# A planned transformer block on one NeuronCore: another written-out issue order, with the second norm's scale and shift of chunk 3 done for pairs of tiles

## The chip, the cores and the metric

The kernel runs on one core of a Trainium2 chip. Five engines work side by side, each through its own list of instructions in a fixed order: TensorE (PE) does matrix products, VectorE (DVE) and ScalarE (ACT) work element by element, GpSimd (POOL) does a little of the same more slowly, and SyncE (SP) issues nearly all DMA transfers. An instruction starts when its turn in its engine's list has come and the results it needs are there; a late one holds up everything behind it on that engine. The metric is the device time of one execution in microseconds (us), the median of several runs; lower is better.

## The reference, cut to what matters

All tensors are bf16; there are S = 2048 tokens of D = 512 numbers, 32 heads of 16, F = 1792.

```python
sa, ca, ga, sb, cb, gb = six rows of (silu(c) @ w_mod)
h = layernorm(x) * (1 + ca) + sa
q, k, v = split(h @ wqkv)                     # 32 heads of 16
logits[s, w] = q[s] . k[s - 2 * w] / 4        # w = 0..7, masked where s - 2w < 0
x = x + ga * ((softmax(logits) . v[s - 2 * w]) @ wo)
h = layernorm(x) * (1 + cb) + sb
h = layernorm(h)                              # the mixer's own norm
u = gelu(h^T @ w1 + b1)                       # over the tokens: [512, 2048] @ [2048, 1792]
x = x + gb * (u @ w2 + b2)^T
```

Each token attends to eight earlier ones, two apart. The second half mixes the tokens: its first product needs the normed rows of all 2048 tokens before any of its results is complete, and its second product needs all of `u`.

## The kernel before, in words

The 2048 tokens are 16 tiles of 128, and the tiles form five chunks of 2, 4, 4, 4 and 2 tiles (`SIZES`; chunk 0 has tiles 0 and 1, chunk 1 has tiles 2 to 5, chunk 2 tiles 6 to 9, chunk 3 tiles 10 to 13, chunk 4 tiles 14 and 15). `build_chunk` (line 605) lists the operations of one chunk by name. In each name the first number is the chunk or the tile:

- `ln1s`, `rstd1_`, `nb1_`, `n1_`: the first norm. VectorE takes mean and variance of a tile (a statistics instruction and an aggregate), ScalarE makes the reciprocal root of a group, VectorE makes the bias `nb`, and the tile is scaled and shifted (`n1_`) on ACT, DVE or POOL. Which one is written down per tile in the strings `NE` (line 265: first, second and third norm; A, D, P).
- `tr`/`hT` or `xt`: the tile is transposed, by TensorE and copies in chunks 0 and 1, by DMA in chunks 2 to 4.
- `qkv`, `ev`: products with the weights, which `wsc` has scaled by `1 + ca` (column `a1col`, from `modcols1`, from the loaded `ld_wmod1`); results are moved from PSUM to SBUF by `ev`.
- `qk`, `red`, `max`, `sub`, `exp`, `esum`, `rcp`, `smB`: the logits. VectorE multiplies q by the eight shifted k (`qk`, four instructions a chunk, 128x4096 in chunks 1 to 3 and 128x2048 in chunks 0 and 4); TensorE sums over the head's numbers (`red`), and the softmax follows.
- `vd`, `a2`: DMAs that lay out v and the softmax for the next step. `pv`, `pvacc`, `oev`: VectorE multiplies softmax by v, TensorE sums, ACT moves the result. `wo`, `x1`: the output product and the new x.
- `ln2q`, `ln2m`, `rstd2_`, `nb2_`, `n2_`: the second norm (mean and square sums on ACT, `ln2m` turns them into mean and variance on DVE). `aff`: VectorE multiplies by `1 + cb` and adds `sb` (two instructions), for a group of `GRP[ch]` tiles. `ln3s`, `rstd3_`, `nb3_`, `h3_`: the third norm.

The token mixer's first product (`mlp1_<sweep>_<f tile>_<first token tile>`) runs in sweeps over ranges of token tiles (`MIX`), so that TensorE has work on finished tiles while later chunks are still in attention: sweep 0 over tiles 0 to 5 or 0 to 9, parked in SBUF by `park`, later sweeps added by `inj` or `padd`; then `gelu`, and `mlp2` with `fin` and the store `st_out`. The weights of the mixer come in by `ld_w1_` (three buffers in rotation) and `ld_w2_`.

Nothing is scheduled while the kernel is built: `ORDER` (line 182) is the issue order of all operations written out, `schedule` (line 85) follows it, hands out buffers by it (six PSUM banks, four product buffers `big`, five `vD`) and lets every engine's list fall out of it. A token `:a`, `:d` or `:p` picks the engine where there is a choice; `:q` splits a product into four that use 32 columns of the array each; `fill:k:n` puts n small products on TensorE that compute nothing (`warm` does the same). Every instruction is recorded at line 133, the helper that issues it, so the profile is read by tile names and by order.

Of the kernel before, what the change touches and what calls it, by code (L numbers as in the profile page):

```python
# [179 lines left out]


ORDER = """
ld_x_1_2 ident ld_c act_table ld_x_1_4 ld_x0 consts warm2 ld_x_2_8 ld_x1 cps ld_x_2_6 silu_exp ld_wmod1 ln1s3
ld_wqkv1 ln1s5 ld_wqkv0 ld_x_3_10 ln1s4 ln1s2 ln1s0 rstd1_1 ln1s1 ld_wmod0 ln1s9 rstd1_0 nb1_0 nb1_1 silu_dve
n1_1 n1_0 ld_x_4_14 ln1s6 n1_5 n1_2 fill:2:114 tr0_0 ln1s8 modcols1 n1_3 halo0 ld_wqkv2 n1_4 hT0_3:a hT0_1:d
hT0_0:a ld_x_3_12 fill:4:11 tr1_2 a1col hT0_2:d wsc1_0:a wsc1_1:d tr1_0 ld_wo3 wsc1_3:d wsc1_2:d hT1_3:a ln1s7
qkv0_12 hT1_1:a ld_wmod5 wsc0_0:a wsc0_1:d qkv0_10 wsc0_3:d ld_b2 rstd1_2 wsc0_2:d ln1s10 ld_wmod4 hT1_0:a
qkv0_00 ev0_10:a ln1s11 ev0_12:a modcols0 ld_wo0 nb1_2 qkv0_02 sab hT1_2:d ld_wmod3 n1_6 qvb0 ln1s15 qkv1_02
qvb_cp0 ln1s14 wsc2_2 ev0_02:a qvb1 ln1s13 wsc2_3 qkv1_10 wsc2_1:a wsc2_0:a qvb_cp1 qk0_3 qkv1_00 ev0_00:a
qkv0_22 qk0_2 ev1_02:a qkv1_01 ev1_10:a qk0_0 qkv0_20 ev1_01:a qk0_1 ev1_00:a red0_0 xt6 qkv1_12:q n1_9 qk1_0  # L190
ev0_20:a red0_1 red0_2 ld_wo1 red0_3 mask ev1_12:a ld_wmod2 qkv1_13:q n1_7 qkv1_03 max0 n1_8 xt7 qk1_2 qkv1_11
ev1_03:a xt9 sub0 qkv1_23 ev1_11:a exp0 qkv1_21 qk1_1 ev1_13:a xt8 ev0_22:a esum0 qkv1_22:q ld_b1 rcp0 halo_v1:p
rstd1_4 vd0_1 smB0 qkv1_20 qk1_3 a2_0_1 modcol2 a2_0_0 ev1_20:a red1_0 ev1_23:a a2_0_2 red1_1 ev1_22:a red1_2
a2_0_3 ln1s12 red1_3 ev1_21:a ld_wo2 qkv2_00 mcols0 nb1_4 max1 rstd1_3 n1_14 vd0_0 n1_15 qkv2_10 vd0_2 nb1_3
ev2_00:a n1_10 sub1 pv0_1 ev2_10:a xt10 qkv2_01 n1_12 qk2_0 mrowt0 qkv2_02 exp1 vd1_3 qkv2_11 vd0_3 ev2_01:a
n1_11 vd1_2 qkv2_22 pv0_2 ev2_11:a xt12 qkv2_12 mrows0:a ev2_02:a qk2_1 pvacc0_2 xt11 ev2_12:a red2_0 n1_13
esum1:q halo_v2:p xt13 qkv2_13:q rcp1 qk2_2 ev2_22:a qkv2_03:q vd1_1 ev2_13:a qkv2_23:q ev2_03:a smB1 qkv2_20:q
qk2_3 a2_1_3 red2_1 ev2_20:a a2_1_2 qkv3_01:q halo_k3:a ev2_23:a a2_1_0 red2_2 a2_1_1 qkv3_13 pv0_0 ld_w1_0_896
red2_3 st_row0 pv0_3 ev3_13:a qkv2_21:q vd1_0 max2 pvacc0_0 ev2_21:a qkv3_10:q pv1_3 pvacc0_1 sub2:q oev0_0:a
qkv3_23:q ev3_10:a exp2 qkv3_00:q ld_row0 pv1_2 xt14 ev3_01:a qkv3_02:q ev3_00:a qkv3_20:q vd2_0 ev3_23:a vd2_1  # L200
esum2:q pv1_0 ld_w1_0_0 qkv3_21 rcp2 pvacc0_3 qkv3_03:q woq_s oev0_2:a ev3_02:a pvacc1_3 ev3_03:a smB2 qkv3_11:q
pv1_1 a2_2_2 wo1:q ev3_11:a a2_2_1 ev3_21:a wo0 xt15 x1_1 halo_v3:a qk3_1 pvacc1_1 oev1_3:a a2_2_0 pvacc1_0 x1_0
a2_2_3 qkv3_12 oev1_1:a ld_w1_0_512 oev1_0:a qk3_0 pvacc1_2 vd2_2 modcol3 oev1_2:a vd2_3 ev3_12:a ln2q0 wo4
qk3_3 wo5 x1_4 ln2q1 qkv4_12 mcols1 ev3_20:a qk3_2 red3_0 ln2q4 red3_1 qkv3_22:q ln2m0 wo3 ev3_22:a pv2_1 x1_5
mrowt1 wo2:q mrows1:a x1_3 st_row1 red3_2 pv2_0 x1_2 pvacc2_1 rstd2_0 red3_3 ln2q2 qkv4_02:q oev2_1:a ld_row1
nb2_0 max3 n2_0 vd3_3 ev4_02:a vd3_0 pv2_3 sub3 vd3_2 qkv4_10 exp3 pvacc2_0 n2_1 esum3 pv2_2 ln2q3 qkv4_20
ev4_12:a qkv4_22:q rcp3 ev4_20:a ln2m2 pvacc2_2 aff0 warm3 oev2_0:a oev2_2:a qkv4_00:q smB3 rstd2_2 ln2q5 nb2_2
pvacc2_3 ln3s0 a2_3_1 n2_2 warm1 ev4_22:a a2_3_0 ln3s1 n2_3 biascols oev2_3:a a2_3_2 ln2m4 ev4_10:a aff2 wo7:q
a2_3_3 rstd2_4 ld_w2_1 rstd3_0 wo6:q nb2_4 nb3_0 ln3s2 n2_4 n2_5 h3_0 vd3_1 ln3s3 wo8:q h3_1 x1_6 aff4 warm0
rstd3_2 x1_7 wo9:q nb3_2 ln3s4 h3_2 h3_3 x1_8 ln3s5 halo_v4:p mlp1_0_2_0:q vd4_1 ev4_00:a pv3_0 mlp1_0_5_0:q  # L210
x1_9 mlp1_0_1_0:q rstd3_4 ln2q9 mlp1_0_0_0:q nb3_4 pv3_3 biascols_cp:a vd4_2 h3_5 pvacc3_0 h3_4 mlp1_0_6_0:q
ln2q8 mlp1_0_0_4:q pv3_2 mlp1_0_1_4:q vd4_3 park0_0:a mlp1_0_5_4:q mlp1_0_2_4:q park0_1:a mlp1_0_4_0:q ln2q7
park0_2:a pv3_1 mlp1_0_3_0:q vd4_0 ln2q6 mlp1_0_3_4:q oev3_0:a pvacc3_2 park0_3:a ld_w1_0_1152 pvacc3_3 oev3_2:a
ln2m6 mlp1_0_4_4:q qk4_0 oev3_3:a pvacc3_1 rstd2_6 mlp1_0_7_0:q oev3_1:a nb2_6 qk4_2 red4_0 n2_9 mlp1_0_6_4:q
wo13:q n2_7 qk4_1 ld_w1_0_1408 n2_6 wo12:q qk4_3 n2_8 park0_4:a red4_1 red4_2 aff6 red4_3 ld_w2_3 park0_5:a
wo11:q x1_12 mlp1_0_9_0:q ln2q12 park0_6:a wo10:q max4 x1_11 ld_w2_0 ln3s8 x1_13 sub4:q mlp1_0_10_0 ln3s7 exp4
x1_10 ln3s6 esum4 mlp1_0_11_0 ln3s9 rcp4 mlp1_0_12_0 smB4 rstd3_6 ln2m12 a2_4_3 ln2q10 h3_7 mlp1_0_8_0 h3_6
a2_4_1 rstd2_12 h3_8 mlp1_0_8_4 ln2q13 a2_4_2 nb2_12 h3_9 n2_12 ln2q11 a2_4_0 ln2m13 mlp1_0_9_4 ln2m10 rstd2_13
aff12 mlp1_0_7_4 rstd2_10 nb2_10 ln2m11 mlp1_0_7_8 ln3s12 rstd2_11 mlp1_0_8_8 n2_10 mlp1_0_9_8 pv4_0
ld_w1_0_1664 mlp1_0_11_4 park0_7:a rstd3_12 nb2_13 pv4_2 mlp1_0_10_4 park0_8:a n2_13 mlp1_0_10_8 nb2_11 pv4_1  # L220
mlp1_0_11_8 park0_9:a ld_w1_1_0 mlp1_0_12_4 park0_10:a pv4_3 mlp1_0_12_8 park0_11:a pvacc4_2 pvacc4_0 park0_12:a
aff10 pvacc4_1 pvacc4_3 n2_11 mlp1_0_13_0 aff13 ld_w2_5 oev4_0:a mlp1_0_13_4 aff11 oev4_2:a mlp1_0_13_8 inj1_0
wo15 ln3s10 wo14 ln3s13 rstd3_10 ln3s11 park0_13:a mlp1_1_0_6 x1_15 ld_w1_1_640 rstd3_13 ld_w1_1_896 rstd3_11
ln2s15 inj1_4 inj1_2 inj1_3 mlp1_1_3_6 nb3_13 h3_10 rstd2_15 nb2_15 mlp1_1_2_6 x1_14 n2_15 ln2s14 h3_13
mlp1_1_3_10 inj1_1 mlp1_1_0_10 mlp1_1_1_6 aff15 rstd2_14 nb2_14 mlp1_1_2_10 ln3s15 n2_14 mlp1_1_4_6 park1_0:a
h3_12 mlp1_1_1_10 aff14 inj1_5 rstd3_15 inj1_6 mlp1_1_4_10 mlp1_1_5_6 ln3s14 ld_w1_1_1408 mlp1_1_6_6 h3_11
rstd3_14 h3_15 park1_1:a h3_14 mlp1_1_6_10 mlp1_1_5_10 park1_2:a mlp1_1_10_10 ld_w1_2_0 park1_3:a mlp1_1_9_10
# [12 lines left out]

# [1 line left out]
def kernel(  # L242
# [19 lines left out]
    NA2: int = 2,  # L262
    NB=2,
    NH2=2,
    NE=('PAPADADAAADAAAPA', 'AAPPAPAAAAAAPAAA', 'APPAAADDDDDDDADD'),
    X1D=(14, 15),
    LN2D=(14, 15),
    GRP=(2, 2, 4, 1, 1),
    XDMA=(2, 3, 4),
    INJ=(1,),  # L270
    WARM=4,
# [47 lines left out]
    mask = T([32, NW, PAD], BF, "mask")  # L319
# [11 lines left out]
    ident = T([P, P], BF, "ident")  # L331
    group4 = T([P, 32], BF, "group4")
    epscol = T([P, 1], F32, "epscol")
    a1col = T([P, KT], F32, "a1col")
# [8 lines left out]
    sab = T([P, KT], BF, "sab")  # L343
# [32 lines left out]
    def ln_rstd(l, g0, n, name, var=None, vreads=None):  # L376
# [228 lines left out]
    def build_chunk(ch):  # L605
# [205 lines left out]
        for st in tiles:  # L811
# [206 lines left out]
```

## Time and profile before

| | us |
|---|---|
| median of 3 runs | 207.13 (206.99 to 207.7) |
| the profiled execution | 206.99, of which span 205.1 |
| first product with the scaled weights | 13.35 |
| first logit product on VectorE (`qk0_3`) | 20.32 |
| `nb3_2`, which lets the third norm of tiles 2 and 3 start | 91.49 |
| end of the last `pv` (`pv4_3`) | 123.45 |
| last product's start, end of the last store | 201.17, 204.30 |

| stretch, us | PE busy | DVE busy | ACT busy | POOL busy |
|---|---|---|---|---|
| 0 to 13.3 | 11.60 | 8.74 | 5.95 | 3.82 |
| 13.3 to 91.5 | 75.08 | 77.05 | 62.21 | 9.74 |
| 91.5 to 123.5 | 31.41 | 31.08 | 29.50 | 1.81 |
| 123.5 to 199 | 75.50 | 42.18 | 20.35 | 0.00 |

TensorE's clock was granted in full throughout (1.00). A busy TensorE is not one at its peak: products are pipelined, and their ends are modelled. So TensorE is read here by starts: from one operation's start to the next one's. A 512-column product takes 0.216 us that way (`mlp2` of one tile: 14 products in 3.02 us).

### The profile page before, as it was taken

Reading aid. Unit: us, or ns where it says so; the run is one execution under the profiler, and the core shown is the slowest. Engines: PE = TensorE matmul, PEld = TensorE weight load, DVE = VectorE, ACT = ScalarE, POOL = GpSimd, SP = SyncE. Lnnn points to the kernel's source line nnn. Section 1 sums busy time; section 2 is a strip of 40 time slices with the busy share of each in tenths; the row PEclk is TensorE's granted clock in tenths of the full one; section 3 lists DMA queues with packets and bytes.
Section 4 is the critical chain, followed back from the end, with each engine's and each line's share of the span. In section 5 each row is a group of like instructions: output and inputs, shape, how many; then the busy total and the mean of one; then the engine's idle time right before and its main releaser. Section 6 shows DMA issues by size and latency. Waiting matters only on the chain.

```text
span 205.1 us, 5082 instructions
## 1 busy us (share of the span) xinstructions
PE 196.7 (96%) x2089; PEld 106.7 (52%) x2089; DVE 162.6 (79%) x258; ACT 118.0 (58%) x271; POOL 15.4 (7%) x36
## 2 busy tenths in 40 slices
PE   7999999997999997999999999999999999999994
PEld 6988654453553644644555444444444444444453
DVE  2989999999999999999999899964563262066845
ACT  2396897983768788989999796673682000000000
POOL 4112007120000000230000100000000000000000
PEclk9999999999999999999999999999999999999999
DMA  5999684796859839073389149559992045006202
GB/s 170 303 375 298 156 174 113 219 261 183 247 180 283 243 141 357 27 190 147 121 220 219 27 97 336 187 125 291 274 300 67 29 135 146 0 26 165 81 26 78
DMA packets 55114, 35.98 MB, mean 175 GB/s; under 512 B 24628, under 2 KB 52404, under 8 KB 55092
## 3 DMA queue, kind: packets, MB, share of 16 engines
q1 hardware_dynamic: 55084, 35.67, 63.1%
q8 instruction: 16, 0.26, 0.5%
q14 instruction: 6, 0.05, 0.1%
q10 hardware_dynamic: 8, 0.00, 0.0%
HBM read 22.55 MB, written 2.10 MB: 120 GB/s over the span
## 4 chain that ended last, share of the span: by engine, by line
PE 52%; DVE 31%; issue 6%; ACT 5%; DMA 3%; SPq 2%; DVEq 0%
PE psS L133 50%; DVE big L133 17%; DVE h L133 5%; DVE st L133 4%; DVE mv L133 2%; PE psL L133 2%; ACT h L133 2%; SPq L133 2%; DMA xx<-in_A_x_dram 1%; DMA a2sb<-lsb 1%; ACT xx L133 1%; DVE lsb L133 1%; DVE m L133 1%; ACT q_sb L133 1%; DVE nb L133 0%
## 5 line engine op out<-in xcount | busy, mean ns | idle before, releaser
L133 PE MATMUL psS<-h,wst 128*32 128x512 bf16 (+1 forms) x374 | 51.1, 379 | 0.4 <-POOL h L133 0.2
L133 PE MATMUL psS<-hT,w_qkv 128*32 128x512 bf16 (+3 forms) x516 | 46.9, 346 | 1.5 <-ACT v_sb L133 1.1
L133 PEld LDWEIGHTS <-wst 128*128 128x128 bf16 (+1 forms) x476 | 29.6, 98 | 30.2 <-issue 2.2
L133 PEld LDWEIGHTS <-w_qkv 128*32 128x32 bf16 (+1 forms) x558 | 29.8, 109 | 22.3 <-issue 3.8
L133 DVE TENSOR_TENSOR big<-a2sb,vD 128x4096 bf16<-128x4096 bf16 (+1 forms) x20 | 36.5, 1861 | 0.2
L133 DVE TENSOR_TENSOR big<-q_sb,k_f 128x4096 bf16<-128x4096 bf16 (+1 forms) x20 | 36.4, 1861 | 0.0
L133 DVE SCALAR_TENSOR_TENSOR h<-psS,bcol,rows_bc 128x512 f32<-128x512 f32 (+2 forms) x18 | 12.4, 691 | 23.2 <-PE psS L133 22.9
L133 PE MATMUL psS<-gT,big 128*128 128x512 bf16 x112 | 24.8, 379 | 0.0
L133 PEld LDWEIGHTS <-ident 128*128 128x128 bf16 (+1 forms) x301 | 15.5, 104 | 6.7 <-issue 2.1
L133 PEld LDWEIGHTS <-big 128*128 128x128 bf16 x144 | 12.0, 98 | 13.2
L133 ACT ACTIVATE h<-xx,nb,rs 128x512 bf16<-128x512 bf16 x22 | 17.2, 808 | 1.7 <-DVE nb L133 1.7
L133 PE MATMUL psS<-woq,o_sb 128*32 128x512 bf16 (+1 forms) x184 | 16.5, 380 | 0.4 <-ACT xx L133 0.4
L133 DVE TENSOR_TENSOR psS<-psS,gT 128x512 f32<-128x512 f32 x14 | 9.0, 694 | 8.0 <-PE psS L133 8.0
L133 DVE BATCH_NORM_STATS2 st<-xx 128x6 f32<-128x512 bf16 x18 | 12.2, 677 | 3.8 <-DMA xx<-in_A_x_dram 3.7
L133 ACT ACTIVATE v_sb<-psS,qvb 128x512 bf16<-128x512 f32 (+1 forms) x20 | 11.2, 598 | 4.3 <-PE psS L133 4.2
L133 ACT ACTIVATE lv<-mv,epscol 128x1 f32<-128x1 f32 (+2 forms) x25 | 7.3, 292 | 11.0 <-DVE mv L133 10.8
L133 PE MATMUL psS<-ident 128*128 128x128 bf16 x161 | 12.0, 242 | 1.4 <-POOL epscol L133 1.4
L133 ACT ACTIVATE q_sb<-psS,qvb 128x512 bf16<-128x512 f32 (+1 forms) x20 | 11.1, 599 | 2.8 <-DVE qvb L133 1.9
L133 DVE TENSOR_TENSOR h<-h,xx 128x512 bf16<-128x512 f32 (+2 forms) x18 | 11.4, 632 | 1.6 <-DMA out_dram<-h 1.0
L133 ACT ACTIVATE gT<-psS,bcol 128x512 bf16<-128x512 f32 x14 | 8.7, 684 | 7.0 <-DVE psS L133 7.0
L133 DVE TENSOR_TENSOR h<-h,rows_bc 128x512 bf16<-128x512 bf16 (+2 forms) x20 | 11.5, 581 | 0.3
L133 PEld LDWEIGHTS <-group 128*32 128x32 bf16 x288 | 7.0, 96 | 8.8 <-issue 2.7
(89 smaller groups left out, 213.9 us busy)
## 6 DMA issues: line engine op xcount, KB each, us to landing
vD<-v_sb SPq DMA_DIRECT2D x12, 524.5 KB, 4.6
big<-in_B_w_dram SPq DMA_DIRECT2D x4, 896.0 KB, 8.1
vD<-v_sb SPq DMA_DIRECT2D x8, 268.5 KB, 2.6
wst<-in_B_w_dram SPq DMA_DIRECT2D x3, 640.0 KB, 4.4
out_dram<-h SPq DMA_DIRECT2D x15, 128.0 KB, 1.8
xx<-in_A_x_dram SPq DMA_DIRECT2D x7, 256.0 KB, 6.9
wst<-in_B_w_dram SPq DMA_DIRECT2D x2, 800.0 KB, 4.8
gT<-in_w_mod_dram SPq DMA_DIRECT2D x3, 512.0 KB, 8.3
```

The source lines that it names most:

```text
L133: r = fn(*a, **k)
```

## The change

The operations are almost the same; their order and their engines differ.

- `ORDER` is replaced as a whole. The order of the x loads and of the modulation and weight loads on SP, the order within every chunk on VectorE, and which products are quartered (50 before, 59 after) all change.
- `GRP[3]` goes from 1 to 2: in chunk 3 the second norm's scale and shift, and the statistics' root and bias, are made for tiles 10 and 11 together and for 12 and 13 together.
- `NE` changes the engine of some norms. First norm: POOL has tiles 2, 3, 5 and 15 (before 0, 2 and 14), DVE tiles 1 and 10 (before 4, 6 and 10). Second norm: POOL has 0, 3, 5, 12 and 14 (before 2, 3, 5 and 12). Third norm: tiles 10, 11 and 15 go from DVE to ACT.
- `halo_k3` and `halo_v3` (copies of 16 columns) go to POOL, `halo_v2` and `halo_v4` to ACT; `wsc2_1` goes from ACT to DVE, `park1_1` and `park1_3` from ACT to DVE.

```diff
 ORDER = """
-ld_x_1_2 ident ld_c act_table ld_x_1_4 ld_x0 consts warm2 ld_x_2_8 ld_x1 cps ld_x_2_6 silu_exp ld_wmod1 ln1s3
-ld_wqkv1 ln1s5 ld_wqkv0 ld_x_3_10 ln1s4 ln1s2 ln1s0 rstd1_1 ln1s1 ld_wmod0 ln1s9 rstd1_0 nb1_0 nb1_1 silu_dve
-n1_1 n1_0 ld_x_4_14 ln1s6 n1_5 n1_2 fill:2:114 tr0_0 ln1s8 modcols1 n1_3 halo0 ld_wqkv2 n1_4 hT0_3:a hT0_1:d
...
-qvb_cp0 ln1s14 wsc2_2 ev0_02:a qvb1 ln1s13 wsc2_3 qkv1_10 wsc2_1:a wsc2_0:a qvb_cp1 qk0_3 qkv1_00 ev0_00:a
...
-ev4_12:a qkv4_22:q rcp3 ev4_20:a ln2m2 pvacc2_2 aff0 warm3 oev2_0:a oev2_2:a qkv4_00:q smB3 rstd2_2 ln2q5 nb2_2
-pvacc2_3 ln3s0 a2_3_1 n2_2 warm1 ev4_22:a a2_3_0 ln3s1 n2_3 biascols oev2_3:a a2_3_2 ln2m4 ev4_10:a aff2 wo7:q
...
-aff12 mlp1_0_7_4 rstd2_10 nb2_10 ln2m11 mlp1_0_7_8 ln3s12 rstd2_11 mlp1_0_8_8 n2_10 mlp1_0_9_8 pv4_0
...
+ld_x_1_2 ld_c ident act_table ld_x1 ld_x_1_4 consts warm2 ld_x_4_14 ld_x0 cps ld_wmod1 ld_wqkv1 ln1s3 halo0
+ld_x_2_8 ln1s2 ld_wqkv0 ln1s4 ln1s1 ln1s5 ld_x_2_6 ln1s0 rstd1_1 silu_exp nb1_1 ln1s15 rstd1_0 n1_3 ld_wmod0
+nb1_0 silu_dve n1_2 n1_0 ld_x_3_10 n1_1 fill:2:109 modcols1 ln1s14 n1_4 tr0_0 n1_5 a1col wsc1_1:a wsc1_0:d
+ld_wqkv2 hT0_3:d fill:4:10 tr1_0 wsc1_3:d hT0_0:a ld_x_3_12 hT0_2:d hT0_1:a wsc1_2:d rstd1_4 ln1s9 fill:5:7
...
+nb1_2 n1_6 qkv1_12 qvb_cp0 ln1s10 wsc2_3 wsc2_0:a qvb1 wsc2_1:d ev0_00:a nb1_4 wsc2_2 qkv1_10:q qvb_cp1 ln1s13
+n1_8 qkv0_22:q qk0_0 ev0_02:a qkv1_00:q qk0_1 ev0_22:a qkv0_20:q ev1_10:a qk0_2 red0_0 xt6 ev0_20:a qkv1_11:q
...
+pvacc2_3 ev4_22:a ld_w1_0_896 warm3 oev2_1:a ln2m2 pvacc2_0 ln3s1 rstd2_2 oev2_3:a smB3 oev2_0:a nb2_2 ln2m4
+a2_3_1 n2_3 n2_2 wo9:q ln3s0 a2_3_2 rstd2_4 aff2 rstd3_0 a2_3_0 warm0 x1_9 wo7:q a2_3_3 nb2_4 nb3_0 ln3s2 n2_5
...
+nb2_10 pv4_0 ld_w1_0_1664 n2_11 mlp1_0_9_4 park0_8:a pv4_1 n2_10 mlp1_0_10_8 mlp1_0_9_8 aff10 mlp1_0_11_4
+ld_w1_1_0 park0_9:a mlp1_0_11_8 park0_10:a pv4_2 inj1_2 mlp1_0_12_8 park0_11:a mlp1_0_13_0 ld_w1_1_640
...
 """
...
-    NE=('PAPADADAAADAAAPA', 'AAPPAPAAAAAAPAAA', 'APPAAADDDDDDDADD'),
+    NE=('ADPPAPAAAADAAAAP', 'PAAPAPAAAAAAPAPA', 'APPAAADDDDAADADA'),
...
-    GRP=(2, 2, 4, 1, 1),
+    GRP=(2, 2, 4, 2, 1),
```

## The prediction

> **What bounds the kernel now.** I read the page first (engines' shares, then the slices), then the chain, then the stretches between its turning points, then the waits, and last the order of time around GpSimd's few instructions.
>
> ```profile
> span 205.1 us, 5082 instructions
> PE 196.7 (96%) x2089; PEld 106.7 (52%) x2089; DVE 162.6 (79%) x258; ACT 118.0 (58%) x271; POOL 15.4 (7%) x36
> PE   7999999997999997999999999999999999999994
> DVE  2989999999999999999999899964563262066845
> ```
>
> VectorE's 79% is an average over two halves: nines up to slice 24, then much less. TensorE has nines nearly everywhere, but its ends are modelled.
>
> ```profile
> 121.17 2.29 DVE big L133 x2
> 123.46 0.04 issue
> 123.50 75.54 PE psS L133 x355
> 199.04 0.03 issue
> 199.06 0.76 DVE h L133
> ```
>
> The chain says where the hand-over is. Until 123.5 it runs mostly through VectorE's products; from there TensorE does 355 products one after another (0.213 each) with no wait, and a tail of 6.1 (last `fin`, last store) ends it. So the time is: when TensorE gets past `pvacc4_3`, plus what its list still holds, plus a tail.
>
> ```profile
> 13.30:91.50 78.20, 75.08 (x1097) 42.92 (x1101) 77.05 (x93) 62.21 (x141) 9.74 (x9) 1.00 0.78 208
> 91.50:123.50 32.00, 31.41 (x428) 15.61 (x420) 31.08 (x55) 29.50 (x79) 1.81 (x3) 1.00 0.56 146
> 123.50:199.00 75.50, 75.50 (x357) 34.20 (x357) 42.18 (x77) 20.35 (x42) 0.00 (x0) 1.00 0.52 147
> ```
>
> Columns: stretch, length, then busy time of PE, PEld, DVE, ACT, POOL. VectorE is busy 77.05 of 78.20 up to `nb3_2`: it is the clock there, and a wait on it is paid in full. From 91.5 to 123.5 three engines are nearly full.
>
> ```profile
> PE psL L133 <- DVE m L133: 1.5, 1, 1.5
> PE psS L133 <- ACT v_sb L133: 1.1, 1, 1.1
> ```
>
> TensorE's two long waits are short of work that VectorE and ScalarE owe it. Both lie before 91.5; saving them alone gives nothing, since `mlp1` then waits for `h3_2` all the same.
>
> The last view is the order of time, GpSimd against VectorE:
>
> ```profile
> 31.22 3.56 POOL L133 COPY v_sb<-v_sb 128x64 bf16<-128x64 bf16 x1 [11.03 <-ACT v_sb L133]
> ...
> 92.55 0.24 POOL L133 COPY v_sb<-v_sb 128x64 bf16<-128x64 bf16 x1
> 115.56 0.86 POOL L133 TENSOR_SCALAR h<-xx,rs,nb 128x512 bf16<-128x512 bf16 x1 [22.77 <-DVE nb L133]
> ```
> ```profile
> 115.37 0.41 DVE L133 TENSOR_SCALAR h<-h,mv,rs 128x512 bf16<-128x512 bf16 x1
> 115.69 0.15 DVE L133 SCALAR_TENSOR_TENSOR mv<-sums 128x1 f32<-128x1 f32 x1
> 115.95 0.47 DVE L133 TENSOR_TENSOR mv<-mv,sums 128x1 f32<-128x1 f32 x1
> 116.35 0.15 DVE L133 SCALAR_TENSOR_TENSOR mv<-sums 128x1 f32<-128x1 f32 x1
> 116.53 0.16 DVE L133 TENSOR_TENSOR mv<-mv,sums 128x1 f32<-128x1 f32 x1
> ```
>
> The same 128x64 copy takes 0.24 alone and 3.56 when it falls among VectorE's products: it ends at 34.78, just after the last of them (34.69). The other way round, the tiny `ln2m13` product takes 0.47 where its twin takes 0.16, and ends when GpSimd's `n2_12` ends (116.42). The two engines shut each other out, and VectorE can lose.
>
> **The change, part by part.** The sum is made against the profiled execution, 206.99 (span 205.1 and 1.9 around it), 0.14 below the median of 207.13.
>
> Opening, to VectorE's first logit product (20.32 before). Up to there both lists hold 15 statistics, 6 weight scalings and 3 `hT` copies on VectorE; the new one has one norm less (0.33 from start to start) and one `nb` more (0.08): 20.07. Its own waits: `hT0_2` still follows `hT0_0` on ACT (0.38 before, 0.3 to 0.4 now, against 0.47 of such waits inside the 20.32), and `qvb_cp0` and `qvb_cp1` come to VectorE 0.25 and 0.15 before TensorE, which has `tr1_2` (0.45) behind `qkv0_12` instead of ahead of it, can deliver. That is 20.37. Then GpSimd: `n1_3`, `n1_2`, `n1_5` (0.76 each, the row of `n1_0`) run from about 8.76 to 11.0, and now VectorE has `nb1_0` and `n1_1` to do there, where it had only statistics before; and `wsc2_3`, `wsc2_2` (18.8 to 20.2) now meet `wsc2_1` on VectorE. The trace doesn't show who gets in between two GpSimd instructions. If VectorE gets in after one, I count 0.15 for `nb1_0`, 0.4 for `n1_1`, 0.05 for `wsc2_1`: 20.95. If nobody waits, 20.37; if VectorE waits for GpSimd's whole row, `n1_1` to 11.05 and `wsc2_1` to 20.2, about 22. I take 20.95, +0.63, as the copy above was kept out of back-to-back products that leave no gap, and GpSimd's do leave one.
>
> The transfers of the opening: the bytes ahead of `wmod1` fall from 1280 to 1024 KB and of `wqkv1` from 1792 to 1536, so `a1col`'s weights land earlier (10.22 for `wmod1` before); `x_2_6` and `x_3_10` move back behind `wqkv0` and `wmod0`. By the landings before (3072 KB at 14.46, 3840 KB at 16.80), `ln1s7` (about 15.6) and `ln1s11` (17.3) still find theirs. Price 0, at worst 0.5 if the cover of 0.5 is gone. ScalarE's `wsc0_2`, `wsc0_0` are about as late as before (`qkv0_00` at 15.41); the fills are 126 products against 125, beside it.
>
> Chunks 0 to 2 in attention, first `qk` to `nb3_2` (71.17 before; the same prices summed over the list give 70.51, so waits and drift are 0.66). The new list is the same work less `nb1_4`, 0.08: the order of `pv` and `qk` is dealt differently, and each product buffer comes free before its turn when I lay TensorE's starts beside VectorE's (tightest: `pv0_0`, whose `a2` transfers land 0.1 to 0.2 after its turn; `pv1_2`, whose `vd1_2` is issued some 4 ahead and took 2.5 to 4.6 in this trace). Same drift: -0.08, bounds -0.6 and +0.5. One new meeting: `ln2m4` now stands directly behind `nb2_2`, and `nb2_2` releases GpSimd's `n2_3`. From the rows, GpSimd starts 0.26 after `nb2_2` starts (85.09 to 85.35), the `ln2m4` product 0.33 after it, so it waits for the 0.76: end at 1.03 + 0.16 minus 0.49 without, some 0.55 to 0.7. I take 0.55; 0 if it slips in first. `aff2` and all behind it on VectorE are late by that.
>
> Third norm to `pvacc4_3`. Before, TensorE lost 1.05 here against the bare sum of its starts: 0.38 for `h3_4`, 0.24 in `red4`, 0.29 before `pvacc4_3`, the rest turns between quartered and whole products (0.11 each; 32 turns in both lists). Now `mlp1_0_0_4` comes after six first halves, not five, which covers `h3_4`; `wo10` waits some 0.1 to 0.4 for `oev3_1`, behind `rstd2_6` on ACT; and `mlp1_0_13_0` and `inj1_2` (0.86 and 0.21) stand ahead of `pvacc4`, so the last `pv` is waited for by nobody. Gain 0.36, bounds 1.0 and 0.
>
> The pairs of chunk 3. `aff` costs 0.80 a tile from start to start alone and 1.33 a pair: 0.54 saved in two pairs; two `ln2m` (0.64) and one `nb` net go; ACT saves four `rstd` (1.8) and gets three norms (2.1) that VectorE gives (1.0). But `aff10` as a pair now stands before `pv4_2`: up to `pv4_3` VectorE's list gets 0.25 longer. All of this lies beside TensorE's backlog: worth 0. What could be late next is `h3_14`, which the products over tiles 10 to 15 need; VectorE has 11.1 after the last `pv` to it (12.9 before), TensorE 11.8 (12.9), so the margin grows by 0.7, of which `nb3_15`'s wait for ACT takes about 0.5. On POOL `n2_14` runs beside statistics, which don't meet it.
>
> Queues. On SP, `ld_w1_0_1664` is issued about 0.8 later and used 1.6 earlier (120.37 landed, used 123.84 before): margin 1.0 left, price 0 to 0.5. `ld_wmod3` and `ld_row0` move behind `vd2_0` and `xt15` and still have some 2 before `woq_s`; `ld_w2_0` holds SP until `qkv4_12` (about 79), past `vd3_3`, which `pv3_3` needs at 97. On POOL `halo_k3` will hang until `max2` (about 53) and `halo_v3` behind it; `qk3_3` (56.7) and `vd3_2` (74) wait later than that: 0, and if `max2`'s gap weren't enough, +2. `mlp2` and the last `fin`, store: the same lengths, 0.
>
> Sum: 0.63 - 0.08 + 0.55 - 0.36 = +0.74, so 207.73 for a profile, 207.87 beside the median. I say 207.8.
>
> A rule against this part of the change: the Trainium skill, "SBUF — State Buffer", section "Who interferes with whom", says that a VectorE instruction with two SBUF inputs or in a two-port mode and a GpSimd instruction that reads SBUF take the shared port pair whole, the first to start wins, and statistics or a reduction don't take part. The two long rows above agree with it. By the rule all four meetings happen, and the sum is the +0.74; without it, by the bare list, it would be -0.39.
>
> **The rivals.** (a) Nobody waits: GpSimd's and VectorE's instructions miss each other. For it: `n1_0` and `n1_2` ran beside `silu_dve` before at no cost. Against: `ln2m13`. Then 0.05 - 0.08 - 0.36 = -0.4: 206.7; with TensorE's whole 1.05 saved, 206.0. This one ends on the faster side. (b) VectorE waits for whole rows of GpSimd: the opening ends at 21.5 to 22, +1.3 to +1.8: 208.5 to 209. For it: the copy that got in nowhere for 3.5. (c) A transfer is late: the displaced x tiles, `a2`, `vd1_2` or `w1_0_1664` have 0.1 to 1.0 of margin each; one that is 1 to 2 late adds that, since VectorE or TensorE has nothing else in its list: 208.5 to 209.7. (d) The change doesn't do what it says: the distance from a weight's issue to its product is shorter for `w1_0_1664` (4.5 for 6.9). As no product waited for weights before, longer distances win nothing; this changes no number, and it holds beside the others.
>
> **How the numbers follow.** A measurement tells about 0.3% here, 0.62 us. Chances: likeliest (each meeting costs once) 0.40, own range 207.3 to 208.4; (a) 0.30, 206.0 to 207.4; (b) 0.18; (c) 0.12. Faster (below 206.5) has two thirds of (a): 0.20. Same (to 207.75) has the rest of (a) and four tenths of the likeliest: 0.26. Slower: 0.54. Range 205.9 to 209.5: the whole of (a) at the low end, one late transfer at the high end, and the unknown costs inside.
>
> **What would show it.** Right: `n1_1`, `wsc2_1` and the `ln2m4` product longer than 0.41, 0.35 and 0.16; the first `qk` at about 20.9; `nb3_2` at about 92.6; `mlp1` after it with less than 0.7 of waits; TensorE unbroken after `pvacc4_3`; a 6.1 tail. Wrong: first `qk` before 20.5 and `nb3_2` before 91.6; or a wait of over 0.5 on TensorE for a DMA; or for `h3_14`.

## The result and the profile after

| | before | after |
|---|---|---|
| median, us | 207.18 (6 runs, 206.94 to 207.7) | 209.49 (6 runs, 208.66 to 209.77) |
| ratio, 95% interval | | 1.0103 [1.0081, 1.0124] |
| profiled execution, span | 206.99, 205.14 | 209.61, 207.87 |
| first logit product on VectorE | 20.32 | 20.52 (+0.20) |
| from there to `nb3_2` | 71.17 | 73.99 (+2.82) |
| from `nb3_2` to the last product's start | 109.68 | 109.40 (-0.28) |
| from there to the end of the span | 3.97 | 3.96 (-0.01) |

The change made the kernel 1.0% slower, and nearly all of the profile's +2.73 lies in the stretch from the first `qk` to `nb3_2`. Four of the kernels below had one execution each in a slower state of the chip; it is left out of their medians and ratios. Four lines of the page of after:

```profile
span 207.9 us, 5244 instructions
PE 197.9 (95%) x2180; PEld 109.0 (52%) x2180; DVE 162.6 (78%) x248; ACT 117.4 (56%) x263; POOL 15.9 (8%) x38
...
PEclk9999969999999999999999999999999999999999
...
q8 instruction: 17, 0.28, 0.6%
```

TensorE has 91 products more (59 quartered ones for 50), one slice has a clock digit of 6, and queue q8, of the kind "instruction", has 17 packets where the page of before had 16. The stretches of after that answer to the ones shown of before (columns as there):

```profile
13.30:94.50 81.20, 76.53 (x1190) 45.78 (x1193) 77.34 (x91) 63.36 (x142) 8.89 (x10) 0.98 0.76 205
94.50:127.45 32.95, 32.56 (x439) 15.62 (x429) 31.67 (x49) 28.72 (x71) 1.63 (x2) 1.00 0.62 154
127.45:203.00 75.55, 75.55 (x366) 34.83 (x363) 42.21 (x76) 19.95 (x39) 0.77 (x1) 1.00 0.48 136
```

VectorE, which was the clock up to `nb3_2`, now idles 3.86 of 81.20 there, against 1.15 of 78.20. The waits of after say where:

```profile
PE psS L133 <- issue: 2.0, 1, 2.0
DVE big L133 <- ACT q_sb L133: 1.8, 1, 1.8
...
DVE m L133 <- PE psL L133: 1.3, 1, 1.3
```

The chain of after runs through the first of them (its longest pieces, in order of time):

```profile
13.21 9.86 PE psS L133 x182
23.08 1.99 issue
25.69 0.87 PE psS L133 x16
...
113.98 90.89 PE psS L133 x481
```

At 23.08 TensorE stops for 1.99 us, and nothing that the profile knows holds it. Second by second, after first and before second (columns as in the stretches; the last three are TensorE's granted clock, the DMA engines' share and GB/s):

```profile
22.00:23.00 1.00, 1.00 (x35) 0.71 (x27) 1.00 (x2) 1.00 (x4) 0.00 (x0) 1.00 0.50 128
23.00:24.00 1.00, 0.08 (x3) 0.00 (x0) 1.00 (x2) 0.23 (x1) 0.00 (x0) 1.00 0.10 35
24.00:25.00 1.00, 0.00 (x0) 0.00 (x0) 1.00 (x1) 0.00 (x0) 0.00 (x0) 1.00 0.00 0
25.00:26.00 1.00, 0.93 (x21) 0.91 (x25) 0.13 (x1) 0.48 (x2) 0.00 (x0) 1.00 0.00 0
26.00:27.00 1.00, 1.00 (x20) 0.79 (x13) 0.04 (x1) 1.00 (x3) 0.58 (x2) 0.71 0.29 63
27.00:28.00 1.00, 1.00 (x15) 0.75 (x11) 1.00 (x1) 1.00 (x3) 0.40 (x1) 0.50 0.69 90
```
```profile
23.00:24.00 1.00, 1.00 (x13) 0.80 (x15) 1.00 (x2) 0.86 (x2) 0.00 (x0) 1.00 0.28 82
24.00:25.00 1.00, 1.00 (x21) 0.49 (x21) 1.00 (x2) 1.00 (x2) 0.00 (x0) 1.00 0.06 19
```

After a second of 35 matmuls TensorE goes silent, ScalarE runs dry behind it, and from 25 to 27 VectorE does 0.17 of 2. Then the granted clock is 0.50 from 26.41 to 29.82. What lands in the silence is shown by the DMA view of after, cut to 22.7 to 23.9:

```profile
q8 instruction: 1, 0.02, 5.7%
```

The trace's packets put it at 22.77 to 23.86: 16384 bytes of instructions. So the first theory, F: TensorE ran out of instructions. It stopped after the 705th record of its list (matmuls, weight loads and three of its sequencer). Its list is the denser the more products are quartered, and its next packet stood in the queue of the opening's loads (loads issued at 14.85 and 15.49 landed at 23.86 and 24.19, the packet at 23.86). The rivals: G, the loss comes from the new order and GpSimd's meetings; C, it comes from the halved clock.

### The profile page after: what moved, and what is told of

It is laid out like the page before. It is cut to its first block, busy times and chain, and to the rows that moved or that the text cites. A ratio compares the mean times of both kernels' runs of the same rounds, so it can differ in the third digit from the quotient of the medians.

```text
span 207.9 us, 5244 instructions
## 1 busy us (share of the span) xinstructions
PE 197.9 (95%) x2180; PEld 109.0 (52%) x2180; DVE 162.6 (78%) x248; ACT 117.4 (56%) x263; POOL 15.9 (8%) x38
## 4 chain that ended last, share of the span: by engine, by line
PE 71%; DVE 13%; ACT 5%; DMA 5%; issue 3%; SPq 2%; DVEq 0%; ACTq 0%
PE psS L133 68%; DVE big L133 5%; PE psL L133 3%; DVE h L133 2%; DVE st L133 2%; ACT h L133 2%; DMA a2sb<-lsb 2%; DMA xx<-in_A_x_dram 2%; SPq L133 2%; DMA vD<-v_sb 1%; DVE lsb L133 1%; DVE mv L133 1%; ACT junk L133 1%; DVE m L133 1%; ACT lsb L133 0%
## 5 line engine op out<-in xcount | busy, mean ns | idle before, releaser
L133 PE MATMUL psS<-hT,w_qkv 128*32 128x512 bf16 (+3 forms) x660 | 49.0, 355 | 2.4 <-issue 2.0
L133 PEld LDWEIGHTS <-w_qkv 128*32 128x32 bf16 (+1 forms) x702 | 32.5, 110 | 22.2 <-issue 4.0
L133 ACT ACTIVATE h<-xx,nb,rs 128x512 bf16<-128x512 bf16 x21 | 16.5, 808 | 2.4 <-DVE nb L133 2.4
L133 POOL TENSOR_SCALAR h<-xx,rs,nb 128x512 bf16<-128x512 bf16 x9 | 7.0, 780 | 76.6 <-DVE nb L133 68.9
L133 ACT ACTIVATE lv<-mv,epscol 128x2 f32<-128x2 f32 (+2 forms) x21 | 6.1, 291 | 10.3 <-DVE mv L133 9.6
L133 DVE TENSOR_TENSOR h<-h,rows_bc 128x1024 bf16<-128x1024 bf16 (+2 forms) x16 | 11.0, 688 | 0.5 <-ACT h L133 0.2
```

What stands on the lines that cost most here:

```text
L133: r = fn(*a, **k)
```

## The experiments

Ratios are to the kernel before on the same chip, where its median was 207.8 to 208.05 with single runs from 206.8 to 209.2. A difference of 0.5 between two single profiles therefore means little; the medians of five to twelve runs and the waits themselves carry the verdicts.

### Why TensorE stopped

**Two products whole.** The order of after, two tokens changed:

```diff
-qkv0_22:q   -qkv0_20:q
+qkv0_22     +qkv0_20
```

> The changed kernel with two of its early quartered products whole again (qkv0_22 and qkv0_20: 16 instructions each on TensorE's list instead of 64). Theory F: TensorE stood from 23.08 to 25.07 because its list's next instructions were still on their way (the trace has a 16384-byte instruction packet at 22.77 to 23.86, and TensorE stopped after its 705th instruction); 96 instructions fewer mean that the 705th is reached at about 25.3 instead of 23.1, after the packet has landed, so the 2.0 stall, VectorE's gaps of 1.83 before qk1_0 and 1.28 before max0 go: nb3_2 at 91.5 to 92.0 instead of 94.51, time 206.8 to 207.4 against 209.49. Rival G: the loss between 25 and 31 comes from the new order itself (GpSimd's n1_15 and the order of evictions): the gaps stay, 209 to 209.5. Rival C: the loss is the granted clock of 0.5 from 26.4 to 29.8, and the stall alone is covered: the time moves only as far as the clock, and runs with clock 1.00 are at 208.7 to 209.8 already, so no change.

Measured: 208.26, ratio 1.0007 [0.9985, 1.0029]. The stop is gone, and VectorE's gaps before `qk1_0` and `max0` with it. Changing two tokens of the order brings back the 1%, within the interval. `nb3_2` came at 93.23, not 91.5 to 92.0: a wait that the stop had covered appeared in its place.

```profile
DVE big L133 <- DMA a2sb<-lsb: 1.2, 1, 1.2
```

**One product whole.**

```diff
-qkv0_22:q
+qkv0_22
```

> The changed kernel with only qkv0_22 whole: 48 instructions fewer ahead of the stop. Theory F: the 705th instruction is reached at about 24.1 instead of 23.1, the packet lands at the same time as before (23.9) and TensorE goes on 1.2 after it: a stall of about 1.0 instead of 2.0, now ahead of red0_2 instead of inside qkv0_20, and about half of the 2.3 is lost: 207.9 to 208.6. Rival G: 209 to 209.5, as nothing about GpSimd or the evictions changes. If the stall is tied to qkv0_20 itself (its buffer or its operands), it stays 2.0 at the same place.

Measured: 207.91, ratio 1.001 [0.998, 1.004]; two of the eleven runs compared took 209.8 and 209.9, the others 206.8 to 208.3. TensorE stopped for 0.44 (25.14 to 25.58), inside `qkv1_11` instead of `qkv0_20`, after the very same record of its list, the 705th. The stop moved with the count, not with the product:

```profile
24.33 0.82 PE L133 MATMUL psS<-hT,w_qkv 128*32 128x512 bf16 x11
...
25.58 0.41 PE L133 MATMUL psS<-hT,w_qkv 128*32 128x512 bf16 x1 [0.44 <-issue]
```

It was shorter than the 1.0 expected because TensorE had begun 0.58 later (first scaled product at 13.10 for 12.52) and the packet landed only 0.26 later (24.12 for 23.86).

**Six loads later.**

```diff
-ld_wmod5 -ld_wo3 -ld_wo2 -ld_wmod4 -ld_wo1 -ld_b2       (between qkv0_12 and qvb0)
+xt8 ld_wo3 ld_wmod4  +ld_wo0 ld_wo2  +xt7 ld_wo1 ld_b2  +ld_b1 ld_wmod5
```

> The changed kernel with six loads of the opening (wo1 to wo3, wmod4, wmod5, b2) moved behind xt8 and later on SyncE's queue; TensorE's, VectorE's and ScalarE's lists are unchanged, quartered products too. Theory F with the reason that the instruction packet waits behind the loads' backlog like any load (loads issued at 14.9 to 15.5 landed at 23.9 to 24.2, the packet at 23.9): without 1.4 MB of backlog the packet lands at 19 to 21.5, TensorE doesn't stop, 206.8 to 207.4 unless one of the moved loads comes late for its product. If the packet's time is set by TensorE's own progress and not by the backlog, it stays at 22.8 and the stall at 2.0: 209.5. Rival G: 209 to 209.5.

Measured: 213.3, ratio 1.0255 [1.0226, 1.0284]. The packet came at 18.59, 4.2 earlier, and TensorE didn't stop, with every product quartered as in after. TensorE passed its 449th record, 256 ahead of the 705th, at 17.3 to 18.4 in all fourteen profiles of this study; the packet began 0.9 to 1.2 later in the four kernels with loads moved back (this one and three below) and 2.5 to 5.5 later in the other ten. So the backlog is what made the packet late. The time was lost elsewhere, to my own moves: VectorE waited 5.0 for the softmax's transfers (`pv0_0` 2.36, `pv1_3` 1.22, `pv4_0` 1.45). The loads that now stood ahead put SyncE behind: it issued the first `a2_0` 2.9 after `smB0` had ended and the first `a2_1` 1.2 after `smB1`. The transfers for `pv1_3` and `pv4_0` also had an instruction packet among them (52.52 to 53.45, 121.03 to 122.29).

**The kernel before with six products quartered.**

```diff
-qkv1_02 qkv1_10 qkv1_00 qkv0_22 qkv1_01 qkv0_20
+qkv1_02:q qkv1_10:q qkv1_00:q qkv0_22:q qkv1_01:q qkv0_20:q
```

> The kernel before with six early products quartered (qkv1_02, qkv1_10, qkv1_00, qkv0_22, qkv1_01, qkv0_20: 192 instructions more on TensorE's list ahead of red0_0; nothing else changed). Theory F: the 705th instruction comes at about 23.0 instead of 30.0, the instruction packet still starts at about 21.8 and lands at 23.1, TensorE goes on at 24.2 to 24.3: a stall of 1.2 to 1.3, and a time of 207.6 to 208.6 against 207.18. Rival G: quartering the same work costs nothing here, 206.9 to 207.4.

Measured: 210.45, ratio 1.0108 [1.0063, 1.0153]. TensorE stopped for 1.05 after its 705th record, 1.33 after the packet's end at 23.62 (1.21 in after, 1.46 with one product whole), and the clock stayed at 1.00:

```profile
24.95 1.07 PE L133 MATMUL psS<-hT,w_qkv 128*32 128x256 bf16 x32 [1.06 <-ACT q_sb L133]
...
26.35 2.29 DVE L133 TENSOR_TENSOR big<-q_sb,k_f 128x4096 bf16<-128x4096 bf16 x1 [1.04 <-PE psL L133]
```

The profile puts the stop down to ScalarE's q, but `ev0_00`, the step that `qkv0_20` needs, had ended at 21.94. The time rose by more than the stop explains: the last softmax transfers landed 3.7 and 4.1 after their issue, `pv4_0` waited 1.37 for them and TensorE 0.58 and 0.73 behind it. That became the second question.

So F holds for the stop: it goes and comes with the quartered products, in both kernels; it keeps to the count; and it goes when the queue is cleared. The kernel before had a late packet too (21.81 to 23.05), but its list reached the 705th record at 29.95 only. C falls as the cause of the loss: four of the six runs of after had a clock of 1.00 and took 208.66 to 209.77. The Trainium skill, "TensorE: Matmul & The Clock Gate", section "Part 1: The HAM clock gate (the "warmup" mystery)", says that an idle window of about 3.4 us halves TensorE's clock. The length of the one dip agrees, 3.41 at 0.50; the stop ahead of it was shorter than such a window, 1.99, so here less was enough.

### What the stop had covered

**The next packet moved.** On top of the two products:

```diff
-qkv1_13:q   -qkv1_20:q
+qkv1_13     +qkv1_20
```

> The first experiment's kernel (two early products whole) with qkv1_13 and qkv1_20 whole too: 48 instructions fewer on TensorE's list, at a place where TensorE has slack. There the next instruction packet came at 34.71 to 36.02, right on the issue of a2_0_0, which took 1.72 instead of 0.61 and ended 0.43 after the packet; pv0_0 then waited 1.20 on VectorE for the softmax's transfers. Theory R (a packet on its way holds SyncE's issue until 0.4 after its end): the packet now comes at 36.2 to 36.7, behind the four a2_0 (issued by 35.9); pv0_0 waits at most 0.2, and the time goes down by about 1.0 from 208.26, ratio to before about 0.996. Rival: the a2_0 transfers are late because the queue is full of the x transposes and the loads; then pv0_0 waits 1.0 to 1.3 as before and the ratio stays 1.000.

Measured: 207.86, ratio 0.9993 [0.9971, 1.0015]. The packet moved to 36.25 as forecast, and the four `a2_0` went out unhindered (2.68 for four, against 3.78); it was `vd1_1` whose issue now took 1.25. But `pv0_0` still waited 1.13. By 35.60 + 2.04 the last `a2_0` should have been there at 37.65, 0.15 after VectorE's turn; it was usable at 38.6. The packet now stood across the transfer itself. So the packet seems to cost in two ways, of which the theory had one; the time that it promised, some 1.0, did not come. SyncE's issues of the two kernels, with two products and with four whole:

```profile
33.32 3.78 SPq L133 DMA_DIRECT2D a2sb<-lsb  x4
37.21 1.20 SPq L133 DMA_DIRECT2D vD<-v_sb  x2
```
```profile
33.53 2.68 SPq L133 DMA_DIRECT2D a2sb<-lsb  x4
36.32 1.89 SPq L133 DMA_DIRECT2D vD<-v_sb  x2
```

**The x load of tiles 4 and 5 first,** and `vd1_2` earlier:

```diff
-act_table ld_x1 ld_x_1_4      -xt12 xt13 xt11 ... xt14 ... vd1_2
+act_table ld_x_1_4 ld_x1      +xt12 vd1_2 xt13 xt11 ... xt14
```

> As the kernel with the packet moved, and two moves on SyncE's queue: the load of x tiles 4 and 5 ahead of that of x tile 1 (as in the kernel before), and vd1_2 three transposes earlier, ahead of xt13. In four runs with the changed kernel's opening VectorE waited 0.2 to 0.8 for that x load before ln1s4, and first qk came at 20.52 to 21.15. If that load is the opening's loss, the wait goes (to below 0.1), first qk comes at 20.1 to 20.4, and the time is 0.3 to 0.6 below that of the kernel with the packet moved alone: ratio 0.993 to 0.994. If the opening's loss is GpSimd meeting VectorE, as the prediction had it, first qk stays at 20.7 or later. The waits of 0.45 to 0.57 at pv1_2 or pv1_3 go or stay with vd1_2: at most another 0.5.

Measured: 207.84, ratio 1.0009 [0.9986, 1.0031], a miss. VectorE's wait before `ln1s4` went, but in the profiled run the opening's transfers behind landed later (x tiles 6 and 7 at 15.79; 13.8 to 14.5 in the runs with two, one and four products whole), and first `qk` came at 21.83. Whether the swap or chance delayed them, one profile can't tell. `pv1_2` and `pv1_3` waited for nothing, but so it was in the kernel that this one starts from. The opening stays open to about 0.5.

**The pairs alone,** in the kernel before (`GRP` 2 for chunk 3; the single steps' names go, the pair's stand at the later one's place):

```diff
-    GRP=(2, 2, 4, 1, 1),
+    GRP=(2, 2, 4, 2, 1),
-ln2m12 ... rstd2_12 ... nb2_12 n2_12 ... ln2m13 ... aff12 ... pv4_0 ... pv4_2 ... pv4_3 ... aff10 ... aff13 aff11
+... ln2m12 ... ln2m10 rstd2_12 ... rstd2_10 nb2_12 n2_12 ... pv4_0 ... aff12 pv4_2 ... pv4_3 ... aff10
```

> The kernel before with pairs in chunk 3 alone (the second norm's group of two tiles; the names of the single tiles' steps drop out of the order, the pair's stand where the later of the two stood; engines as before). The prediction's step: VectorE saves about 1.2 us and ScalarE 1.8 in a stretch where TensorE has a backlog, so 0: ratio 0.998 to 1.002. If the pairs' longer steps ahead of pv4 delay the last attention step on VectorE by the 0.2 to 0.5 that they are longer, TensorE waits before pvacc4_3: 1.001 to 1.003. If VectorE's savings count: 0.995.

Measured: 208.86, ratio 1.0046 [1.002, 1.0071]. Not free: VectorE stood 0.26 to 0.72 four times between 116.7 and 119.3 (for ScalarE's sums and roots and for `a2_4`), `pv4_3` came later, and TensorE waited for it:

```profile
PE psS L133 <- DVE big L133: 1.3, 3, 0.7
```

In this profile `nb3_2`, ahead of all pairs, came 0.91 later than before as well, so it doesn't price them; the medians do. In after `mlp1_0_13_0` and `inj1_2` stand ahead of `pvacc4`, and TensorE's list is unbroken there; that the pairs would cost as much without these two is not shown.

**The changed kernel once more.**

> The changed kernel itself, beside the others on one chip. Theory F: TensorE stops after its 705th instruction until 1.2 to 1.5 after the packet's end, for 1.2 to 2.5 according to when the packet lands, whatever the clock does; ratio 1.008 to 1.012. Rival C (the half clock after the stop makes the loss): if the profiled run keeps a clock of 1.00, VectorE's gaps before qk1_0 and max0 are below 1.0 together and the run is as fast as before.

Measured: 209.2, ratio 1.0081 [1.0051, 1.0111]. The profiled execution is its fastest (208.28): there the packet came at 20.92 to 22.25, 1.85 earlier than in the first profile of the same kernel, and TensorE didn't stop. So the forecast of a stop was missed in this profile, and with no stop there was nothing to tell F from C. From the first `qk` to `nb3_2` it took 72.29, against 73.99 with the stop and 71.17 before: the stop is worth about 1.7, one profile against one. How many of the unprofiled runs stopped is not known. What this one met is the same wait as in the first experiment:

```profile
DVE big L133 <- DMA a2sb<-lsb: 1.5, 1, 1.5
```

### Packets placed

**Ten products whole, two issues behind the `a2_0`.**

```diff
-qkv1_10:q qkv0_22:q qkv1_00:q qkv0_20:q qkv1_11:q qkv1_03:q qkv1_02:q qkv1_01:q qkv1_13:q qkv1_20:q
+qkv1_10 qkv0_22 qkv1_00 qkv0_20 qkv1_11 qkv1_03 qkv1_02 qkv1_01 qkv1_13 qkv1_20
-ld_wo0 ... -vd0_3
+a2_0_2 vd0_3 ld_wo0
```

> The changed kernel with its ten early quartered products of chunks 0 and 1 whole (as most of them are in the kernel before), and with vd0_3 and the load of wo0 behind the four a2_0 on SyncE's queue. In the kernel with the packet moved pv0_0 still waited 1.13: the packet at 36.25 to 37.30 fell into the last a2_0 transfer (issued 35.60, usable at 38.6 instead of 37.65). If that is so, here the packet comes at about 40, the a2_0 are issued from 33.0 to 35.8 and pv0_0 waits at most 0.2: ratio 0.993 to 0.997. If the wait has another cause (the transposes' traffic), pv0_0 waits 0.9 to 1.4 again and the ratio stays at 0.999 to 1.001.

Measured: 209.32, ratio 1.0055 [1.003, 1.0079]. `pv0_0`'s wait went to nothing as forecast, and the packet came at 40.55; but SyncE, behind with its list by then, issued the first `a2_1` at 48.43 only, 2.08 after `smB1` had ended; the next packet (51.09 to 51.97) fell on the last of them (issued 50.64, landed 53.92), and `pv1_3` waited 2.15. The wait removed was won and lost again some 14 us later. That the packet at 40.55 put SyncE behind is only argued.

**Two loads late.**

```diff
-ld_wmod5 -ld_wmod4
+vd0_1 ld_wmod5   +xt13 ld_wmod4
```

> The changed kernel with only two loads of the opening later on SyncE's queue (wmod5 behind vd0_1, wmod4 behind xt13, 1 MB together, needed at 68 us); every product is quartered as in the changed kernel. If the packet waits in the backlog of the loads, it comes about 2.5 earlier, at 19.5 to 21, and TensorE doesn't stop at its 705th instruction: ratio 1.000 to 1.003, as with the two products whole. If quartering itself costs the time, 1.008 to 1.010.

Measured: 210.21, ratio 1.0087 [1.0056, 1.0119]. The ratio missed the 1.000 to 1.003 and is the one named for the rival, that quartering itself costs the time. The trace speaks against the rival: the packet came at 18.42, TensorE didn't stop, and `nb3_2` came at 92.66 for 94.51, with 1.63 of waiting at `pv1_3` ahead of it. (The next kernel, with the ten products quartered too, is as fast as before.) The rest was lost again, and the last loss is plain in the timeline of that kernel:

```profile
121.22 2.36 DVE L133 TENSOR_TENSOR big<-a2sb,vD 128x2048 bf16<-128x2048 bf16 x2 [1.56 <-DMA a2sb<-lsb]
...
126.10 0.62 PE L133 MATMUL psS<-big,group 128*32 128x256 bf16 x16 [1.24 <-DVE big L133]
```

A packet at 118.69 met the last `a2_4`, issued at 117.39: it landed after 3.71. In the fourteen profiles the transfers of that group (chunk 4) whose landing the trace has land 2.02 to 2.05 after the start of their issue, except in three: 3.60 in the one with six loads later, 3.71 and 4.13 in the one with six products quartered, and here 3.71, 3.18 and 2.17. In each of the three a packet began with one of them on its way (the 3.18 here had none); in the others none did, but for two that began within 0.35 of the landing and cost nothing.

**Packets placed.** If packets cost by what they meet, their times can be chosen, since each comes at roughly a fixed count of instructions:

```diff
-ld_wmod5 -ld_wmod4              -qkv2_10:q -qkv2_02:q -qkv2_00:q
+ld_wmod3 ld_wmod5 ld_wmod4      +qkv2_10 +qkv2_02 +qkv2_00
```

> The changed kernel with the loads of wmod5 and wmod4 behind wmod3 (issued at about 57 instead of 12 to 15), and three products of chunk 2 whole (qkv2_10, qkv2_02, qkv2_00: 72 instructions fewer on TensorE's list from about 36 on). In the run with two loads late the opening's packet came at 18.42 and TensorE didn't stop, but a packet at 48.43 met the a2_1 transfers (pv1_3 waited 1.63) and one at 118.69 the last a2_4 (landed 3.7 after its issue instead of 2.0; pv4_0 waited 1.56 and TensorE 1.24). If packets cost by what they meet, these two now come at about 51 and 121 to 126, behind the transfers; the three waits go below 0.4 each, nb3_2 comes at 91.0 to 91.8, pvacc4_3 at 123.7 to 124.5, and the ratio to before is 0.990 to 0.997. If the waits came from the two loads' own traffic or from the order, pv1_3 or pv4_0 still waits over 1 and the ratio is 1.000 or more.

Measured: 207.74, ratio 0.9995 [0.9977, 1.0013]. The waits and stages came as forecast: no wait for `a2` at all, `nb3_2` at 91.42, `pvacc4_3` at 124.08, the last product's start at 200.81 (203.91 in after, 201.17 before). The stretch up to `nb3_2` and the row of `pv0_0`, which follows on `n1_10` without a gap:

```profile
13.30:91.40 78.10, 74.51 (x1146) 43.10 (x1157) 77.00 (x91) 63.65 (x142) 10.79 (x10) 1.00 0.79 212
```
```profile
37.18 0.41 DVE L133 TENSOR_SCALAR h<-xx,rs,nb 128x512 bf16<-128x512 bf16 x1
37.51 3.49 DVE L133 TENSOR_TENSOR big<-a2sb,vD 128x2048 bf16<-128x2048 bf16 x3
```

The ratio was missed all the same. A 17th packet, at 201.58 to 202.54, met the last stores: the issue of `st_out15_1` took 1.13 for 0.33, and the end came 4.55 after the last product's start, for 3.97.

**The last packet.**

```diff
-qkv2_00
+qkv2_00:q
```

> The kernel with the packets placed, with qkv2_00 quartered again (24 instructions more on TensorE's list). There a last instruction packet at 201.58 to 202.54 met the last stores: the issue of st_out15_1 took 1.13 instead of 0.33 and st_out15_2 was issued at 203.00, 2.25 after the last product's start (1.69 in the kernel before). With 24 instructions more the packet comes some 2.5 earlier, at about 199, ahead of the last stores. If a packet costs by what it meets, st_out15_2 is issued at most 1.8 after the last product's start, and the time falls by 0.4 to 0.5: 207.2 to 207.4 against 207.74, ratio 0.996 to 0.998. If the end was late for another reason, the ratio stays at 0.999 to 1.001. The packets at 53 and 126 come 1 and 2.5 earlier, still behind the a2_1 and a2_4 transfers.

Measured: 207.52, ratio 0.998 [0.9961, 0.9999]: 0.2% below before, at the edge of what can be told, and just above the 207.2 to 207.4 expected. The last store was issued 1.69 after the last product's start, as in the kernel before; read the same way, from the product and not from its weight load, the run without the change had 2.19. But with 24 instructions more the sixth packet came at 49.43 to 51.04 instead of 53.51, on the last `a2_1` (landed 4.10 after its issue), and `pv1_3` waited 0.73.

## Why the prediction was right, and where it was wrong

The direction was right (slower had 0.54), and 209.49 lies inside 205.9 to 209.5, by 0.01. Both are luck more than insight: the likeliest sum had +0.74 over the profiled execution, made of meetings with GpSimd that mostly weren't there, and the measured +2.62 came from a cause that stood in none of its parts.

- **First `qk` to `nb3_2`, "same drift: -0.08, bounds -0.6 and +0.5".** Measured +2.82, of which the stop is about 1.7 by the two profiles of the same kernel; the one without it had 1.46 of waiting for `a2` at `pv0_0`. This is the step that failed, and in it the sentence that each product buffer comes free in time "when I lay TensorE's starts beside VectorE's". I had laid TensorE's starts as if its list were always there. The quartered products, ten of them with no whole one between, I counted as turns of 0.11 and not as instructions: 16 products and 16 weight loads each in chunk 1 and 32 of each in chunk 0, where a whole one has four or eight of each. Nor did I ask what the instructions' own transfers wait for. The page of before had a row for them, q8 with 16 packets, that I passed over.
- **GpSimd's meetings, +0.60 in the opening and +0.55 at `ln2m4`.** Mostly absent. In the profiled run `nb1_0` took 0.14 and `wsc2_1` 0.32, `n1_1` 0.48 for 0.41, `ln2m4`'s product 0.18. In all ten profiles with this order of the opening `n1_1` took 0.48 or 0.49 and `ln2m4`'s product 0.18. `nb1_2`, which I had not listed, was the one that met:

```profile
17.70 1.35 POOL L133 TENSOR_SCALAR w_qkv<-h,a1col 128x512 bf16<-128x512 bf16 x2 [6.54 <-DMA h<-in_A_wqkv_dram]
...
17.86 0.55 DVE L133 SCALAR_TENSOR_TENSOR nb<-mv,rs 128x4 f32<-128x4 f32 x1
...
89.20 0.77 POOL L133 TENSOR_SCALAR h<-xx,rs,nb 128x512 bf16<-128x512 bf16 x1 [7.76 <-DVE mv L133]
89.21 0.18 DVE L133 TENSOR_TENSOR mv<-mv,sums 128x2 f32<-128x2 f32 x1
```

  `nb1_2` takes 0.13 alone; it ended at 18.40, with the first of the two GpSimd instructions (18.39). `ln2m4`'s product has GpSimd's start 0.01 ahead of its own and ran through even so: the cost of the case "0 if it slips in first". `nb1_2` took 0.26 to 0.55 in four of the ten profiles and 0.13 in six; `wsc2_1` took 0.57 to 0.71 in four later runs (one of them with two x loads swapped), where GpSimd's two instructions came later, and 0.32 to 0.34 in the rest. So a fixed price for each meeting was wrong: one never cost anything, others did in some runs and not in others.
- **The opening, 20.95.** 20.52 in the first profile, 20.50 to 21.15 in the nine later ones with this order of loads. The terms as listed add up to 20.97. The number was about right, but not for the reasons given: the x load of tiles 4 and 5 stands behind that of tile 1, and VectorE waited 0.02 to 0.76 before `ln1s4` in nine of the ten profiles with this order of loads, over 0.1 in seven, which I had priced at 0. One came to 20.74 with no such wait and `wsc2_1` at 0.63. What the opening's few tenths are made of stays open.
- **Third norm to the end, -0.36.** -0.28 from `nb3_2` to the last product's start: about right, though not by every step given. TensorE waits for nothing at the last `pv`, as said, and `red4_3` goes from 0.47 to 0.22 from start to start. But `mlp1_0_0_4`, for which six first halves were to cover `h3_4`, waited 0.39 for it (0.20 in before).
- **Pairs, 0.** Right in this order (`nb3_15` waited 0.55, as said), wrong as a statement on the pairs: alone they cost 0.46% [0.20, 0.71].
- **Queues, 0.** `halo_k3` hung as forecast (51.67 to 54.95) at no cost. "`pv0_0`, whose `a2` transfers land 0.1 to 0.2 after its turn" was the right place: 0 here, as the stop had made VectorE late, but 0.89 to 1.46 in four of the profiles without a stop, 2.36 with six loads moved, and 0 in the one with the stop of 0.44 and in the four last ones. Its price had left out the packets.
- **The rivals.** The time fell where (c) had put it, a transfer 1 to 2 late; but none of those that (c) named was it. The late transfer was TensorE's instructions. (a) may be nearer to what the order is worth when few things meet a packet: up to the last product's start the kernel with packets placed was 0.36 ahead of before, one profile against one, for the forecast 0.4; but three of its products are whole and two of its loads moved, so this is not the order alone. (b) didn't happen: the one meeting of after, at `nb1_2`, cost 0.42 and was over with the first of GpSimd's two instructions.

## What to carry to other kernels

Count TensorE's instructions, not only its time: where many small products follow a burst of loads, look at the instruction queue's packets and at the DMA backlog at the moment when the next one is due. A stop with the label "issue", or with a releaser that had long ended, that moves with the count of instructions and not with the product is a late packet; make the products larger there or the loads later. And before crediting an order with a gain, see which short transfers each packet will meet, since a wait removed in one place let the next chain run into one.

## What the runs showed of the hardware

- TensorE's instructions came in packets of 16384 bytes, one for each 256 or so: 16 in the profiles with 4072 to 4264 matmuls and weight loads, 17 in those with 4288 to 4370. The second one began at 21.81 before, when TensorE had started 550 records, at 22.77 and 702 in after, and at 18.4 to 18.6 and 486 or 487 in the four kernels with loads moved later. TensorE stopped after its 705th record in three profiles out of fourteen and went on 1.2 to 1.5 after the packet's end. With the loads moved the next packets began at 695 to 726 and 946 to 971, so by these counts (an inference) the packet that is due when TensorE is past its 449th record brings what follows the 705th.
- The Trainium skill, "Runtime: NRT & Kernel Launch", section "Instruction fetch mechanics", says that each engine's instructions come in 16 KiB blocks of 256 over a queue of its own, and that crossing a block's edge is "mostly hidden". The blocks agree; hidden it was in eleven profiles, and 0.44, 1.05 and 1.99 in three. The page's store of 2048 instructions for TensorE doesn't agree with a stop after the 705th, if it were kept full.
- Of SyncE's 101 copy issues that began with a packet on its way, 47 ended 0.36 to 0.43 after the packet's end (`a2_2_2` of after, issued at 69.49: 1.37, with a packet from 69.14 to 70.45; the median of issues clear of packets is about 0.55); 22 ended before it, so a packet doesn't hold every issue. Chunk 4's transfers of 2.0 took 3.6 to 4.1 where a packet began on their way. In chunk 2 nine clear of packets took 2.14 to 2.25, and 21 on whose way a packet began 2.2 to 5.5. In chunks 1 and 3 some clear ones took 3.0 to 4.3 too, so packets are not the only cause. Which engine or ring they share, the trace doesn't say.
- The opening's landings scatter by 1 to 2 us from run to run (x tiles 6 and 7 land at 12.73 to 14.62 in the ten profiles with one order of x loads), and with them the packet: the same changed kernel stopped in one profile and not in the other.
